# First chunk of w3·w_out in column halves, and the second chunk's transfers held behind the first 256 KB

## The chip, the core and the metric

The kernel runs on one core of a Trainium2 chip. The time is the device time of one launch in microseconds; the runs of a kernel are compared by their medians. A profiled execution is a run of its own, with its own time.

## What is computed

Linear attention without softmax for 8 batches of 8 heads (576 tokens, head dimension 64), an RMS norm over each head's 64 values scaled by `g_norm`, then a feed-forward of two projections multiplied with each other and two more matrices behind them:

```python
def _attn_ref(q, k, v, g_norm):
    kv = np.einsum('bhsd,bhse->bhde', k, v)
    out = np.einsum('bhsd,bhde->bhse', q, kv)
    rms = np.sqrt(np.mean(out * out, axis=-1, keepdims=True) + 1e-06)
    return (out / rms * g_norm).astype(np.float32)
...
    a = x @ w1
    b = x @ w2
    h = a * b @ w3
    return (h @ w_out).astype(np.float32)
```

x has 4608 rows of 512. The weights w1, w2 (512 x 1024), w3 (1024 x 1024) and w_out (1024 x 512) arrive as 64-bit floats. The kernel multiplies w3 by w_out once, at the start, and uses the product (1024 x 512) in place of the two.

## The kernel before

**Stages.** First comes the product of w3 and w_out, here called the fold. It has two halves of 512 rows of w3 (`half` 0 and 1), and each is a sum over eight chunks `c` of 128. In the fold's second half, batch 0 of the attention and the conversion of w1 and w2 are woven in. After that come nine groups of tokens: matrix products in a Strassen-Winograd form (`winograd`), with the attention of the next batch between them, and from the second group on a projection by the folded matrix in the same form (L893). This document is about the first 20 us, the beginning of the fold.

**Loads of a chunk.** `load_next` (L183 to L210) takes the next entry of `todo` and loads it into one of four `raw` buffers of 1 MB. The first eight entries are the chunks c = 0 to 7: 512 KB of w3 and 512 KB of w_out. Chunk 0 comes in four transfers of 256 KB (two of w3, two of column halves of w_out), every other chunk in two of 512 KB. All are issued at L190 by SyncE, in program order; SyncE stands still while one of them waits for its buffer or its semaphore. A semaphore is shared by transfers that lie eight apart in the program, and the later waits for the earlier: chunk 2's transfers wait for the two w3 transfers of chunk 0, and chunk 3's first for chunk 0's first w_out transfer. Four chunks are asked for at once, before anything else.

**Conversion.** The 64-bit words become 32-bit floats in `conversion`. ScalarE takes two instructions for a cut of columns (L152 into a scratch part of `ab`, L153 into `chunks`), VectorE four (L155, L159, L162, L165). `begin_next` issues ScalarE's part, `end_next` VectorE's. Chunk 0 is converted in cuts of 256, 256 and 512 columns, chunk 1 in two of 512, later chunks in one of 1024. In every chunk columns 0 to 511 are w3, 512 to 1023 are w_out. ScalarE's and VectorE's orders are written out by hand here, as are TensorE's, GpSimd's and SyncE's, so each engine works through its list in order.

**Products of a chunk.** `turn_w3` (L583) transposes the four 128 x 128 blocks of w3 on TensorE (L587) into one PSUM bank, and ScalarE copies them to `ab` (L592). `fold_chunk` (L596) multiplies them by the chunk's w_out: four matmuls `m` of 512 columns (L600), each adding to a PSUM bank of its own, so that the four banks collect the sum over the chunks. In the trace each such matmul shows as two MATMUL rows, and each `keep_warm` matmul too.

**Order on TensorE.** 14 matmuls of the identity with itself (`keep_warm`, L265), whose results nobody reads; the four transposes of chunk 0; 5 more of `keep_warm`; a transpose that makes a column of `g_norm` (L1025); three matmuls of chunk 0; the transposes of chunk 1; the fourth matmul of chunk 0; 4 of `keep_warm`; then three matmuls of chunk 1, the transposes of chunk 2, the fourth matmul of chunk 1, and so on.

**Order on ScalarE.** Chunk 0's cuts, the copy of chunk 0's transposes, chunk 1's two cuts, the copy of the `g_norm` column (L1026), chunk 2's one cut, and only then the copy of chunk 1's transposes, without which chunk 1's matmuls can't start. From there on a chunk's conversion alternates with the copy of the chunk before.

Of the kernel before, what the change touches and what calls it, by code (L numbers as in the profile page):

```python
# [11 lines left out]
FP32 = mybir.dt.float32  # L12
# [9 lines left out]
def kernel(  # L22
# [32 lines left out]
    nc = tc.nc  # L55
# [4 lines left out]
    DM = H * D  # L60
    DF = w1.shape[1]
    NP = H // 2
    KF = DF // P
    NH = KF // 2
# [11 lines left out]
    ps_at = ctx.enter_context(tc.tile_pool(name="ps_at", bufs=3, space=PSUM))  # L76
# [5 lines left out]
    def bank(pool, tag):  # L82
        return pool.tile([P, 512], FP32, name=tag, tag=tag)
# [7 lines left out]
    def load_pair(names, b, r):  # L91

        for name in names:
            t = inp.tile([P, 2, J * D], FP32, name=f"{name}_sb")
            nc.sync.dma_start(
                out=t,
                in_=dict(k=k, v=v, q=q)[name][b, 2 * r:2 * r + 2, 0:G, :].rearrange(
                    "h (p j) d -> p h (j d)", j=J
                ),
            )  # L100
            loaded[name, b, r] = t

    def load_kv_left(b):
        for t, src in zip(kv_left, (k, v)):
            nc.sync.dma_start(out=t[0:L], in_=src[b, :, G:S, :].rearrange("h p d -> p h d"))

    def load_q_left(b):
        if b % 2 == 0:
            q_left[b // 2] = inp.tile([P, H, D], FP32, name="ql_sb", bufs=1)
        nc.sync.dma_start(  # L110
            out=q_left[b // 2][(b % 2) * L:(b % 2 + 1) * L],
            in_=q[b, :, G:S, :].rearrange("h p d -> p h d"),
        )
# [64 lines left out]
    raws = []  # L178

    def raw_tile():  # L180
        return conv_pool.tile([P, 1024], w1.dtype, name="raw", bufs=RAW)

    def load_next():  # L183
        if len(raws) == len(todo):
            return
        what, i = todo[len(raws)]
        raw = raw_tile()

        def load(where, src):
            nc.sync.dma_start(out=raw[:, where].rearrange("p (c m) -> p c m", c=src.shape[1]), in_=src)  # L190

        if what == "w":
            for n, w in enumerate((w1, w2)):
                src = w[:, i * P:(i + 1) * P].rearrange("(c p) f -> p c f", p=P)
                load(slice(n * 512, (n + 1) * 512), src)
        elif what == "b":
            for h in range(2):
                src = w3[DF // 2:DF, (2 * i + h) * P:(2 * i + h + 1) * P]
                load(slice(h * 512, (h + 1) * 512), src.rearrange("(m p) f -> p m f", p=P))
        else:  # L200
            src = w3[0:DF // 2, i * P:(i + 1) * P].rearrange("(m p) f -> p m f", p=P)
            cols = w_out[i * P:(i + 1) * P, :].rearrange("p (c f) -> p c f", c=1)

            n = 1 if i else 2
            for h in range(n):
                load(slice(h * 512 // n, (h + 1) * 512 // n), src[:, h * NH // n:(h + 1) * NH // n, :])
            for h in range(n):
                f = slice(h * DM // n, (h + 1) * DM // n)
                load(slice(512 + f.start, 512 + f.stop), cols[:, :, f])
        raws.append(raw)  # L210
# [3 lines left out]
    def conversions(n):  # L214

        what, i = todo[n]
        if what == "w":
            dst = w_sb[:, i].rearrange("p w c f -> p (w c f)")

            return [conversion(n, dst, raws[n], scale=g_col)]  # L220
        if what == "b":
            return [conversion(n, chunks[:, 2 * i:2 * i + 2, 0, :], raws[n])]
        dst = chunks[:, i].rearrange("p w f -> p (w f)")
        cuts = [[0, 256, 512, 1024], [0, 512, 1024], [0, 1024]][min(i, 2)]
        return [conversion(n, dst, raws[n], slice(a, b)) for a, b in zip(cuts, cuts[1:])]

    begun = []
# [1 line left out]
    def begin_next():  # L229
        if len(begun) < len(todo):  # L230
            begun.append(conversions(len(begun)))
            for c in begun[-1]:
                next(c)

    def end_next(load=True):
        for c in begun[len(converted)]:
            all_of(c)
        converted.append(len(converted))
        if load:
            load_next()  # L240

    def all_of(steps):
        for _ in steps:
            pass


    ident = const.tile([P, P], FP32, name="ident")
# [7 lines left out]
    g_col = const.tile([P, 1], FP32, name="g_col")  # L255
# [5 lines left out]
    def keep_warm(n):  # L261

        t = bank(ps_mm, "mm")
        for _ in range(n):
            nc.tensor.matmul(t[:, 0:P], lhsT=ident, rhs=ident, start=True, stop=True)  # L265
# [315 lines left out]
    w3T = {}  # L581

    def turn_w3(half, c):  # L583
        t_ps = bank(ps_at, "at").rearrange("p (m f) -> p m f", m=NH)
        for m in range(NH):
            src = chunks[:, c, 0, m * P:(m + 1) * P]
            nc.tensor.transpose(t_ps[:, m, :], src, ident)  # L587

        w3T[half, c] = ab[c % 4 // 2][:, c % 2].rearrange(
            "p i (a f) -> p (i a) f", f=P  # L590
        )
        nc.scalar.copy(w3T[half, c], t_ps)  # L592

    sums_ps = {}

    def fold_chunk(half, c, ms):  # L596
        if c == 0 and 0 in ms:
            sums_ps[half] = [bank(ps_mm, "mm") for m in range(NH)]
        for m in ms:
            nc.tensor.matmul(  # L600
                sums_ps[half][m], lhsT=w3T[half, c][:, m, :], rhs=chunks[:, c, 1, :],
                start=(c == 0), stop=(c == KF - 1),
            )
            if c == KF - 1:
                nc.scalar.copy(w3o_sb[:, half * NH + m, :], sums_ps[half][m])
# [397 lines left out]
    chunks = fold.tile([P, KF, 2, DM], FP32, name="chunks")  # L1003
    with tc.manual_schedule(
        engines={mybir.EngineType.DVE, mybir.EngineType.Activation, mybir.EngineType.SP}
    ):
        for _ in range(RAW):
            load_next()
        nc.scalar.activation(const.tile([P, 1], FP32, name="warm"), eps_col, AF.Sqrt)
        g_row = const.tile([1, P], FP32, name="g_row")  # L1010
        for e in range(2):
            nc.scalar.dma_start(
                out=g_row[:, e * D:(e + 1) * D], in_=g_norm.rearrange("(o d) -> o d", o=1)
            )


        keep_warm(14)
        begin_next()
        end_next()
        turn_w3(0, 0)  # L1020
        keep_warm(5)
        begin_next()

        g_ps = bank(ps_at, "at")[:, 0:1]
        nc.tensor.transpose(g_ps, g_row, ident[0:1, 0:1])  # L1025
        nc.scalar.copy(g_col, g_ps)  # L1026
        for c in range(KF):

            if c == 0:
                end_next()  # L1030
                begin_next()
            else:
                begin_next()
                end_next()
            if c == 4:
                load_kv_left(0)
                load_pair("kvq", 0, 0)
            elif c == 5:
                load_pair("kvq", 0, 1)
                load_q_left(0)  # L1040
            fold_chunk(0, c, range(NH - 1))
            turn_w3(*((0, c + 1) if c + 1 < KF else (1, 0)))
            fold_chunk(0, c, [NH - 1])
            if c == 0:
                keep_warm(4)


        first = batch(0)
        first.start()
        AT = {1: 0, 2: 1, 4: 2, 5: 3}  # L1050
        norms = {}
        FIRST = len(converted) + KF - 1
        for c in range(KF):
            if c in AT:
                first.begin(AT[c])
                if AT[c] + 1 == NP:
                    load_q_left(1)
            if c - 1 in norms:
                all_of(norms[c - 1])
            if c < KF - 2:  # L1060
                begin_next()

                end_next(len(raws) < FIRST)
            elif c == KF - 2:
                run(sum_w(0))
            else:
                run(combine_x(0))
                end_next(False)
                for _ in range(3):
                    load_next()  # L1070
            fold_chunk(1, c, range(NH - 1))
            if c + 1 < KF:
                turn_w3(1, c + 1)
            fold_chunk(1, c, [NH - 1])
            if c in AT:
                if AT[c] % 2:
                    norms[c] = first.product(AT[c] // 2)
                    next(norms[c])
                    next(norms[c])
            if c - 1 in norms:  # L1080
                first.turn(AT[c - 1] - 1)
                first.turn(AT[c - 1])
# [88 lines left out]
```

## Time and profile before

| | |
|---|---|
| runs | 781.51, 781.77, 780.90, 780.05 us, median 781.21 |
| profiled execution | 782.82 us, its span 781.0 us |
| mean granted TensorE clock in it | 0.993 |
| TensorE weight loads busy | 662.7 us, 85% |
| VectorE busy | 543.6 us, 70% |
| ScalarE busy | 251.0 us, 32% |
| GpSimd busy | 129.2 us, 17% |
| share of the ended-last chain on TensorE | 90% |
| the same, on DMA | 4% |

A page of the profile gives busy times by engine, the chain of work that ended last, and groups of instructions. The chain is followed back from the last instruction to whatever released each step, so a piece of it is time that nothing else hid in that execution. The timeline of one engine lists its instructions in order: start, duration, engine, line, operation, the tile written and the tile read, shapes, how many were merged, and in brackets how long the engine sat idle before it and what ended that. Times in these views count from the span's start.

### The profile page before, as it was taken

What the parts mean: (1) busy time and instruction counts of PE and PEld (TensorE: products, weight loads), DVE (VectorE), ACT (ScalarE), POOL (GpSimd) and SP (SyncE); (2) the same over time, 40 slices, a digit from 0 to 9 for tenths busy, and PEclk for the clock granted to TensorE, in tenths of its full rate; (3) what the DMA queues carried; (4) which work ended last, traced back from release to release, by engine and by line L of the source; (5) the groups of instructions that cost most, each with busy time, mean ns of one, the idle gap of its engine ahead of it and who ended that gap; (6) DMA issues with size and microseconds to landing.
All of it is one profiled execution on the core that took longest, in us unless ns stands there. A gap on an engine that the chain in (4) does not pass through costs nothing.

```text
span 781.0 us, 14438 instructions
## 1 busy us (share of the span) xinstructions
PE 764.2 (98%) x5787; PEld 662.7 (85%) x5787; DVE 543.6 (70%) x1086; ACT 251.0 (32%) x486; POOL 129.2 (17%) x125
## 2 busy tenths in 40 slices
PE   7999999999979999999999999999999999999996
PEld 5455788888869888988998899889988988898896
DVE  6978999448579557955794778567756864494566
ACT  6687743322211332233223322332133222222120
POOL 0000000111330253024303520341144000000000
PEclk9999999999989999999999999999999999999998
DMA  9996650129987853794389458844841470064024
GB/s 321 327 340 180 194 149 28 55 88 255 256 277 249 243 128 85 282 224 115 74 288 216 119 112 271 205 111 132 275 110 42 141 244 0 1 242 143 1 65 159
DMA packets 129607, 131.76 MB, mean 169 GB/s; under 512 B 73476, under 2 KB 117508, under 8 KB 129540
## 3 DMA queue, kind: packets, MB, share of 16 engines
q1 hardware_dynamic: 127088, 116.02, 50.8%
q10 hardware_dynamic: 2452, 14.81, 5.4%
q8 instruction: 46, 0.75, 0.4%
q14 instruction: 21, 0.17, 0.1%
HBM read 100.27 MB, written 16.38 MB: 149 GB/s over the span
## 4 chain that ended last, share of the span: by engine, by line
PE 90%; DMA 4%; DVE 3%; ACT 1%; SPq 1%; issue 0%; POOL 0%; DVEq 0%; ACTq 0%; POOLq 0%
PE mm L621 57%; PE mm L893 19%; PE mm L600 7%; PE at L326 3%; PE at L409 2%; DMA raw<-w3o_l 2%; DMA raw<-in_moe_w_out_dram 1%; PE at L587 1%; DMA xn<-xT 1%; PE at L345 1%; DVE c L760 1%; DMA w3o_l<-raw 0%; DVE ab L761 0%; PE at L442 0%; DMA raw<-in_moe_w_dram 0%
## 5 line engine op out<-in xcount | busy, mean ns | idle before, releaser
L621 PE MATMUL mm<-xT,w_sb 128*128 128x256 f32 x768 | 176.2, 379 | 0.0
L621 PEld LDWEIGHTS mm<-xT,w_sb 128*128 128x128 f32 x768 | 145.5, 190 | 20.0 <-issue 0.5
L621 PE MATMUL mm<-xc,ws 128*128 128x256 f32 x576 | 132.2, 383 | 4.4 <-ACT p L634 4.4
L621 PEld LDWEIGHTS mm<-xc,ws 128*128 128x128 f32 x576 | 110.4, 192 | 20.0 <-ACT p L634 4.8
L760 DVE TENSOR_TENSOR c<-mm,u 128x512 f32<-128x512 f32 x36 | 24.9, 691 | 109.6 <-PE mm L621 109.6
L634 ACT COPY u<-mm 128x512 f32<-128x512 f32 x74 | 43.3, 585 | 142.9 <-PE mm L621 138.3
L634 ACT COPY p<-mm 128x512 f32<-128x512 f32 x74 | 43.3, 586 | 88.9 <-PE mm L621 79.4
L621 PE MATMUL mm<-xc,w_sb 128*128 128x256 f32 x288 | 69.3, 383 | 0.0
L893 PE MATMUL mm<-w3o_sb,raw 128*128 128x128 f32 x500 | 62.1, 275 | 0.5 <-DVE raw L851 0.4
L600 PE MATMUL mm<-chunks,ab 128*128 128x512 f32 x128 | 60.2, 601 | 2.3 <-DVE chunks L165 2.1
L621 PE MATMUL mm<-xT,ws 128*128 128x256 f32 x256 | 62.0, 386 | 0.0
L761 DVE TENSOR_TENSOR ab<-c 128x256 f32<-128x256 f32 x108 | 58.8, 544 | 3.0
L621 PEld LDWEIGHTS mm<-xc,w_sb 128*128 128x128 f32 x288 | 53.6, 190 | 7.8 <-ACT u L634 0.3
L893 PEld LDWEIGHTS mm<-w3o_sb,raw 128*128 128x128 f32 x500 | 58.8, 192 | 0.8 <-DVE raw L851 0.5
L286 POOL COPY qT<-q_sb 128x1024 uint16<-128x1024 uint16 x24 | 27.4, 1166 | 173.6 <-PE at L409 173.6
L621 PEld LDWEIGHTS mm<-xT,ws 128*128 128x128 f32 x256 | 48.8, 193 | 7.0
L378 DVE TENSOR_REDUCE inv<-sq 128x8 f32<-128x512 f32 (+1 forms) x40 | 23.4, 626 | 42.7 <-ACT sq L377 42.7
L760 DVE TENSOR_TENSOR c<-p,u 128x512 f32<-128x512 f32 x36 | 26.5, 736 | 28.5 <-ACT u L634 28.3
L893 PE MATMUL mm<-w3o_sb,ab 128*128 128x128 f32 x336 | 44.1, 276 | 0.5 <-DVE ab L855 0.3
L893 PEld LDWEIGHTS mm<-w3o_sb,ab 128*128 128x128 f32 x336 | 41.1, 192 | 1.2 <-DVE ab L855 0.5
L600 PEld LDWEIGHTS mm<-chunks,ab 128*128 128x128 f32 x128 | 21.9, 190 | 23.3 <-issue 15.8
L904 ACT COPY u<-mm 128x512 f32<-128x512 f32 x23 | 13.5, 586 | 87.4 <-DVE raw L917 68.4
(160 smaller groups left out, 1140.1 us busy)
## 6 DMA issues: line engine op xcount, KB each, us to landing
w3o_sb<-w3o_l SPq DMA_DIRECT2D x26, 896.0 KB, 5.3
raw<-in_moe_w_dram SPq DMA_DIRECT2D x31, 512.0 KB, 7.1
raw<-w3o_l SPq DMA_DIRECT2D x13, 896.0 KB, 4.8
w3o_sb<-w3o_l ACTq DMA_DIRECT2D x11, 896.0 KB, 4.6
k_sb<-in_k_dram SPq DMA_DIRECT2D x32, 256.0 KB, 4.1
v_sb<-in_v_dram SPq DMA_DIRECT2D x32, 256.0 KB, 4.7
q_sb<-in_q_dram SPq DMA_DIRECT2D x32, 256.0 KB, 4.2
out_dram<-raw SPq DMA_DIRECT2D x14, 512.0 KB, 3.6
```

Source lines behind the costliest of these rows:

```text
L286: nc.gpsimd.tensor_copy(to, words(src).rearrange("p n w -> p w n"))
L326: nc.tensor.matmul(kv_ps[e * D:(e + 1) * D, r - rs[0], :], lhsT=k_sb[:, e, cols] if j < J else kl[:, 2 * r + e, :], rhs=v_sb[:, e, cols] i ...
L345: nc.tensor.transpose(qt_ps[:, e, i, :], q_sb[:, e, i * P:(i + 1) * P], ident)
L378: nc.vector.tensor_reduce(out=inv[:, i], in_=sq.rearrange("p (h d) -> p h d", d=D), axis=AX.X, op=ALU.add)
L409: nc.tensor.matmul(o_ps[l][tokens, n * D:(n + 1) * D], lhsT=qT[r][rows, e, i, tokens], rhs=kv_b[rows, e, r, :], start=True, stop=True,)
L600: nc.tensor.matmul(sums_ps[half][m], lhsT=w3T[half, c][:, m, :], rhs=chunks[:, c, 1, :], start=(c == 0), stop=(c == KF - 1),)
L621: nc.tensor.matmul(ps[:, u, :], lhsT=lhsT(a_name, u, c), rhs=rhs(b_name, c),  start=(u == 0 and c == 0 and to is None), stop=(c == chunks ...
L634: nc.scalar.copy(t, ps)
L760: nc.vector.tensor_add(c, one, two)
L761: nc.vector.tensor_mul(dst, c[:, 0, :], c[:, 1, :])
L893: nc.tensor.matmul(to[:, i, :], lhsT=x[:, c, :], rhs=y[:, c, :], start=new and place // 4 not in seen, stop=(c == 1), skip_group_check=True,)
L904: nc.scalar.copy(t[:, 0:4], ps[0])
```

## The change

Chunk 0 is converted in four cuts of 256 columns. Its four matmuls of 512 columns become eight of 256: first columns 0 to 255 of all four banks, then columns 256 to 511. All eight stand ahead of chunk 1's transposes; before, the fourth matmul stood behind them. `keep_warm(4)` behind chunk 0 becomes `keep_warm(6)`, and the `g_norm` transpose with its copy moves from ahead of chunk 0's matmuls to behind that `keep_warm`. Chunk 1's `raw` buffer gets a GpSimd copy of one column (128 x 1) from chunk 0's buffer. The copy reads what the first transfer of chunk 0 brings, so GpSimd waits for that transfer; chunk 1's first transfer writes over the copied column, so SyncE waits for GpSimd at that transfer. Chunks 2 and 3 stand behind it in SyncE's list.

```diff
         raw = raw_tile()
+        if len(raws) == 1:
+            nc.gpsimd.tensor_copy(raw.bitcast(FP32)[:, 0:1], raws[0].bitcast(FP32)[:, 0:1])
...
-        cuts = [[0, 256, 512, 1024], [0, 512, 1024], [0, 1024]][min(i, 2)]
+        cuts = [[0, 256, 512, 768, 1024], [0, 512, 1024], [0, 1024]][min(i, 2)]
...
-        for m in ms:
+        n = 2 if (half, c) == (0, 0) else 1
+        for h, m in [(h, m) for h in range(n) for m in ms]:
+            cols = slice(h * DM // n, (h + 1) * DM // n)
             nc.tensor.matmul(
-                sums_ps[half][m], lhsT=w3T[half, c][:, m, :], rhs=chunks[:, c, 1, :],
-                start=(c == 0), stop=(c == KF - 1),
+                sums_ps[half][m][:, cols], lhsT=w3T[half, c][:, m, :], rhs=chunks[:, c, 1, cols],
+                start=(c == 0 and h == 0), stop=(c == KF - 1), skip_group_check=True,
             )
...
-        g_ps = bank(ps_at, "at")[:, 0:1]
-        nc.tensor.transpose(g_ps, g_row, ident[0:1, 0:1])
-        nc.scalar.copy(g_col, g_ps)
...
-            fold_chunk(0, c, range(NH - 1))
+            one = NH if c == 0 else NH - 1
+            fold_chunk(0, c, range(one))
             turn_w3(*((0, c + 1) if c + 1 < KF else (1, 0)))
-            fold_chunk(0, c, [NH - 1])
+            fold_chunk(0, c, range(one, NH))
             if c == 0:
-                keep_warm(4)
+                keep_warm(6)
+                g_ps = bank(ps_at, "at")[:, 0:1]
+                nc.tensor.transpose(g_ps, g_row, ident[0:1, 0:1])
+                nc.scalar.copy(g_col, g_ps)
```

## The prediction

> **What bounds the kernel now.** I read the page first, for which engine carries the time.
>
> ```profile
> PE 764.2 (98%) x5787; PEld 662.7 (85%) x5787; DVE 543.6 (70%) x1086; ACT 251.0 (32%) x486; POOL 129.2 (17%) x125
> ```
>
> TensorE works through 98% of the span. What is won or lost in the first 20 us reaches the end only if it moves the point from which TensorE runs without a break. The chain of waits, in order of time, gives that point:
>
> ```profile
> 1.26 3.29 DMA raw<-in_moe_w_dram
> 4.57 8.70 DMA raw<-in_moe_w_out_dram
> 13.38 1.18 ACT ab L152
> 14.55 1.06 ACT chunks L153
> 15.61 0.47 ACT ab L592
> 16.13 2.84 PE mm L600 x6
> 18.97 0.53 PE at L587 x4
> ```
>
> The columns are start, duration and what. From 16.13, chunk 1's first matmul, the chain is TensorE for some 175 us. So 16.13 is the time to watch, and what fixes it isn't chunk 0: it is the w_out transfer of chunk 2, issued at 4.57 and landed at 13.27. ScalarE converts chunk 2 (L152, L153) and only then copies chunk 1's transposes (L592). Later stretches where the chain leaves TensorE (192.76 to 218.71, for example) start from a TensorE result, so they move with it.
>
> Then ScalarE's timeline, for what stands ahead of that copy:
>
> ```profile
> 7.89 0.68 ACT L152 ACTIVATE ab<-raw 128x512 f32<-128x512 uint32 x1 [2.54 <-DMA raw<-in_moe_w_out_dram]
> ...
> 9.02 0.57 ACT L592 COPY ab<-at 128x512 f32<-128x512 f32 x1
> 9.48 0.67 ACT L152 ACTIVATE ab<-raw 128x512 f32<-128x512 uint32 x1
> ...
> 13.38 1.18 ACT L152 ACTIVATE ab<-raw 128x1024 f32<-128x1024 uint32 x1 [1.49 <-DMA raw<-in_moe_w_out_dram]
> 14.46 1.15 ACT L153 ACTIVATE chunks<-raw 128x1024 f32<-128x1024 f32 x1
> 15.52 0.56 ACT L592 COPY ab<-at 128x512 f32<-128x512 f32 x1
> ```
>
> ScalarE waits twice for w_out: 2.54 us for chunk 0's and 1.49 us for chunk 2's. The change is aimed at the first; the second sets 16.13. TensorE's timeline shows how near the two are:
>
> ```profile
> 10.96 2.81 PE L600 MATMUL mm<-chunks,ab 128*128 128x512 f32 x6 [2.14 <-DVE chunks L165]
> 13.61 0.60 PE L587 MATMUL at<-ident,chunks 128*128 128x128 f32 x4
> 14.04 1.02 PE L600 MATMUL mm<-chunks,ab 128*128 128x512 f32 x2
> 14.90 1.05 PE L265 MATMUL mm<-ident 128*128 128x128 f32 x8
> 16.13 2.84 PE L600 MATMUL mm<-chunks,ab 128*128 128x512 f32 x6 [0.17 <-ACT ab L592]
> ```
>
> TensorE idles 2.14 us before chunk 0's matmuls and 0.17 us before chunk 1's. Its own list ends at 15.95, ScalarE's copy at 16.08. An earlier chunk 0 alone is worth 0.17 us of idle time at most, and not that, because the copy ends when it does.
>
> **The transfers.** The trace records when each of a transfer's sixteen shares landed. I count these in the span's time, from the wait that ended at 13.27. Chunk 0's last transfer: fifteen shares between 5.28 and 6.29, the last at 7.80. Chunk 2's w_out: fifteen between 11.19 and 12.23, the last at 13.27. In each transfer from chunk 0's first w_out on, one share is 1.0 to 1.6 us behind the others. It fell behind once, in chunk 0's w_out (5.60 for fifteen, 7.16 for the last; one packet of 2 KB there took 1.12 us, against a mean of 0.10), and the lag stays after that. Landings come in the order of issue, and the engines are busy throughout: by the windows' DMA column 0.85 from 2 to 3 us and 0.89 to 1.14 after. So chunk 2 lands when the latest share has worked off chunks 0 to 2. Asking earlier or later changes nothing, unless a share runs dry.
>
> **The hold, costed.** Chunk 0's first transfer lands at 3.75. GpSimd has been idle since 2.48. The next row for its copy is L548, the same 128 x 1 copy: 0.19 us in the middle, 0.34 at most; the far bound is its large copy at L286, 1.17. From landing to an engine's start the rows give 0.02 (SyncE at 4.57) to 0.11 (ScalarE at 13.38). So SyncE issues chunk 1 at 3.75 + 0.11 + 0.19 + 0.02 = 4.07 instead of 2.81, 1.26 later (dearest 5.05, 2.24 later). I take 0.19, the row of the same shape. Behind it stand chunk 1's w_out (3.29 to 4.55), chunk 2's w3 (3.84 to 5.1) and w_out (4.57 to about 5.6); chunk 3 waits for chunk 0's first w_out (7.16) as before. The first issue, at 0.75, had packets moving at 1.83, 1.08 us later. Chunk 1's packets are thus there from 5.15. The fifteen faster shares are through with chunk 0 between 5.28 and 6.29, the slow one at 7.80: none runs dry. Cost: nothing, covered by chunk 0's own megabyte. Were that cover gone it would be the 1.26 us. Bounds: with the 1.17 us copy packets come at 6.1, the faster shares idle up to 0.85 us, the slowest still not at all.
>
> [...]
>
> **Chunk 0, costed.** The first w_out half (landed 7.16) no longer waits for the second (7.80). ScalarE: chunk 0's first cut of 256 ran from 3.77 to 4.53, 0.76, so the third cut runs 7.25 to 8.0, the fourth 8.05 to 8.8, and the copy (0.57) ends at 9.4; before, 9.59. VectorE: a cut of 256 took 4.24 to 5.66, 1.42, pairs 1.33 apart. Third cut done at 9.05, fourth at 10.36; before, the double cut ended at 10.81. TensorE: eight matmuls of half the columns. A row pair costs 2 x 0.43 at 512 columns in the steady stretch (3.52 for eight rows), so eight half pairs cost 3.45, as four whole ones did; I take no extra for the shorter form (bound: the 128-column row of L265 at 0.13 gives 2 x 0.13 x 16 = 4.2, 0.7 more). They run 9.45 to 12.9. Transposes 0.44, to 13.35. Six `keep_warm` at 1.05/8 per row: 1.58, to 14.9. The `g_norm` transpose 0.22, to 15.1. TensorE then has 0.85 us in hand instead of 0.13, and waits.
>
> ScalarE after its copy of chunk 0: chunk 1's first cut can't start before its w3 lands (9.19), second before w_out lands (10.54), both as before; then it waits for 13.27 as before. Copy of chunk 1 ends 16.08, matmuls at 16.13. The moved copy of the `g_norm` column (0.16) now delays chunk 3's L152 from 16.17 to 16.3; 1.14 us of ScalarE idle at 19.54 hide it. VectorE is 0.45 us earlier until chunk 2, which removes only the weight loads' wait at 18.84, behind TensorE's running matmuls.
>
> Sum: transfers 0, conversion 0 (0.45 gained off the path), TensorE 0 (0.8 gained off the path), copies 0. The span stays 781.0, and the profiled time 782.8. The unprofiled median lay 1.6 below the profiled time; the change concerns nothing that would alter that, so I forecast **781.2 us**, with its own range of 780.6 to 781.8.
>
> **The rivals.** *The late share disappears* (gain). Chunk 0's transfers have the engines to themselves until 5.15. If the 1.12 us stall came from the crowd, chunk 2 lands with its faster shares, at 12.2, the copy ends at 15.0, and TensorE, whose list now ends at 14 to 15, can use it: 1.05 less, 780.1. It is a gain only if the change itself removes the late share: in a run of the kernel before without one, chunk 0 would come early too. Against it: long packets of w_out (0.83, 0.57) appear from 3.5, before chunk 1's first packet. The farthest is set by VectorE, which converts chunks 0 and 1 from landings at 6.3 and ends at about 13.9: 2.2 us less, 779.0.
>
> *The queues run dry* (loss). If the copy on GpSimd or SyncE's wake-up takes longer, or the slow share isn't slow in ordinary runs, the shares wait for chunk 1. It decides from the point where chunk 1's first packet is later than a share's end of chunk 0, so from 6.29 when none is slow, 7.80 when one is. A full loss of the hold is 1.26, 782.5; with the dear copy 2.24, 783.4. For it: the hold is real and everything behind it in SyncE's list is late. Against it: 5.15 lies ahead of all sixteen ends.
>
> *The half-clock stretch moves.* Behind a TensorE idle of 4.39 us at 218.71 the granted clock is 0.50 until 224; eight matmul rows took 3.78 and eight 2.82 there, against 1.89 for such a group elsewhere: 2.8 us. It may fall away or come in a run by its own clock, either sign, 778.4 to 784. I see no reason why the change should steer it.
>
> **How the numbers follow.** Forecast of no change 0.62, the late share gone 0.18, queues dry 0.15, the half-clock stretch 0.05. Nothing over 0.2%, 1.56 us, comes from the forecast itself; 0.2% is about what a measurement of this kernel can tell from no change. Beyond it lie the farther half of the gain and of the loss and the clock: faster 0.13, slower 0.11, within 0.76. The range for 8 in 10 reaches to the near value of the gain and of the loss: 779.9 to 782.5.
>
> **What would show it.** Right: chunk 1's issue at about 4.1, chunk 2's w_out landed near 13.3, ScalarE's second long wait still there, chunk 0's matmuls from 9.5, TensorE idle about 1 us before chunk 1's matmuls at 16.1. Wrong: chunk 1's matmuls a microsecond earlier with no late share, or a DMA column under 0.8 around 5 to 7 us with chunk 2 landing after 14. A wait of TensorE between 20 and 180 us, where there is none now, would break the claim that the end follows 16.13 one for one.

## The result, and the profile after

The changed kernel took 782.60 us in the median (44 runs, 779.76 to 786.54), the kernel before 781.32 in the runs beside it (63 runs, 778.30 to 784.83). The ratio is 1.0018, interval 1.0010 to 1.0026: about 1.3 us slower. The ratios here are those on record, with their 95% intervals; they aren't the quotient of the two medians (1.0016 here), and in samples of 12 runs the two differ by up to 0.0010, so medians stand beside them. The forecast was 781.2, no change. The profiled execution of the changed kernel took 781.13 us, with a span of 779.3; that is less than the 782.82 and 781.0 of the one before, so a reader who compares the two profiles alone gets the wrong sign. Each is one draw from a spread of over 6 us.

The change adds three lines ahead of the functions concerned, and more further down: the matmuls of `fold_chunk` are L606 now, the copy of the transposes L595, `keep_warm` L268, SyncE's issues L193, the column copy on GpSimd L190. First the chain of waits of the changed kernel (start, duration, what):

```profile
3.78 0.02 POOLq L190
3.80 0.10 issue
3.90 0.20 POOL raw L190
4.09 0.02 issue
4.11 0.38 SPq L193
...
5.56 7.86 DMA raw<-in_moe_w_out_dram
...
13.53 1.16 ACT ab L152
14.69 1.04 ACT chunks L153
15.73 0.47 ACT ab L595
16.19 0.07 ACT g_col L1053
16.26 2.83 PE mm L606 x6
```

The hold costs what the prediction's sum said: GpSimd 0.20 us, SyncE's issue at 4.11 where it was 2.81. The chain still goes through chunk 2's w_out, landed at 13.42 (13.27 before), and chunk 1's matmuls start at 16.25 (16.13). On these two traces the change costs 0.12 us.

TensorE's timeline of the changed kernel (start, duration, line, operation, tiles, shapes, and in brackets the idle time ahead and what ended it):

```profile
9.68 3.62 PE L606 MATMUL mm<-chunks,ab 128*128 128x256 f32 x16
13.13 0.60 PE L590 MATMUL at<-ident,chunks 128*128 128x128 f32 x4
13.57 1.50 PE L268 MATMUL mm<-ident 128*128 128x128 f32 x12
15.00 0.22 PE L1052 MATMUL at<-ident,g_row 1*128 1x1 f32 x1
16.25 2.84 PE L606 MATMUL mm<-chunks,ab 128*128 128x512 f32 x6 [1.03 <-ACT g_col L1053]
```

Chunk 0's matmuls start at 9.68 instead of 10.96 with no wait ahead of them. The 2.14 us of idle time that stood there are gone, and 1.03 us stand ahead of chunk 1 instead of 0.17. The idle time has moved, from before work that doesn't set the end to before the work that does. The prediction saw this and costed it at nothing.

The transfers, in the windows of one microsecond (stretch, length, then busy time and instructions of PE, PEld, DVE, ACT and POOL, then the granted clock, the DMA engines' busy share, and GB/s). Before:

```profile
5.00:6.00 1.00, 1.00 (x8) 1.00 (x8) 0.97 (x4) 0.34 (x2) 0.00 (x0) 1.00 0.97 328
6.00:7.00 1.00, 1.00 (x11) 1.00 (x11) 0.91 (x3) 0.00 (x0) 0.00 (x0) 1.00 1.03 337
```

and after:

```profile
5.00:6.00 1.00, 1.00 (x7) 1.00 (x7) 0.97 (x4) 0.29 (x1) 0.00 (x0) 1.00 0.82 177
6.00:7.00 1.00, 1.00 (x6) 1.00 (x6) 0.93 (x4) 0.65 (x2) 0.00 (x0) 1.00 0.81 262
```

One GB/s over one microsecond is 1 KB, so 439 KB arrived in these two microseconds instead of 665, though chunk 1's first packet came at 5.19, as forecast. In windows of half a microsecond the loss lies right behind that packet: 92 GB/s from 5.5 to 6.0 us (344 before) and 180 from 6.0 to 6.5 (360 before), then 344 (313 before). The first transfers of the program rise gradually too: 75, 176, 250, 308 and 377 GB/s in the quarters of a microsecond from 1.75, in the kernel before. That is the loss the prediction excluded with "none runs dry". In this one execution it is nearly hidden, since the late share was gone: of chunk 2's w_out fifteen shares had landed by 13.14 and the last at 13.42, where it had been 12.23 and 13.27. The faster shares lost 0.9 us, and the last nearly nothing: the rival of the late share happened beside the rival of the dry queues, and the two nearly cancelled. Other executions of the same kernel had to show which of them stays.

### The profile page after: what moved, and what is told of

It is laid out like the page before. It is cut to its first block, busy times and chain, and to the rows that moved or that the text cites. A ratio compares the mean times of both kernels' runs of the same rounds, so it can differ in the third digit from the quotient of the medians.

```text
span 779.3 us, 14469 instructions
## 1 busy us (share of the span) xinstructions
PE 764.8 (98%) x5799; PEld 665.4 (85%) x5799; DVE 544.9 (70%) x1090; ACT 251.5 (32%) x488; POOL 129.5 (17%) x126
## 4 chain that ended last, share of the span: by engine, by line
PE 91%; DMA 3%; DVE 3%; SPq 1%; ACT 1%; issue 0%; POOL 0%; DVEq 0%; ACTq 0%; POOLq 0%
PE mm L627 57%; PE mm L899 20%; PE mm L606 7%; PE at L329 3%; PE at L412 2%; DMA raw<-in_moe_w_out_dram 1%; DMA raw<-w3o_l 1%; PE at L590 1%; PE at L348 1%; DVE c L766 1%; DMA xn<-xT 1%; DMA w3o_l<-raw 1%; PE at L445 0%; DMA raw<-in_moe_w_dram 0%; DVE ab L767 0%
## 5 line engine op out<-in xcount | busy, mean ns | idle before, releaser
L767 DVE TENSOR_TENSOR ab<-c 128x256 f32<-128x256 f32 x108 | 60.4, 559 | 3.0
L606 PE MATMUL mm<-chunks,ab 128*128 128x512 f32 (+1 forms) x136 | 59.9, 575 | 1.0 <-ACT g_col L1053 1.0
L606 PEld LDWEIGHTS mm<-chunks,ab 128*128 128x128 f32 x136 | 23.5, 190 | 21.2 <-issue 14.8
```

The costliest lines, as they stand in the source:

```text
L606: nc.tensor.matmul(sums_ps[half][m][:, cols], lhsT=w3T[half, c][:, m, :], rhs=chunks[:, c, 1, cols], start=(c == 0 and h == 0), stop=(c == ...
L767: nc.vector.tensor_mul(dst, c[:, 0, :], c[:, 1, :])
```

## The experiments

Five theories were kept, the last of them only from the trace of `e9_hold_1m_second` on: A, the hold lets the transfer engines run partly dry and chunk 2 lands later; B, the new order and shapes of chunk 0 cost the time; C, the difference is chance; D, the time is lost later in the program; E, an idle stretch of TensorE just ahead of chunk 1 halves its clock in some executions. All kernels here compute the full result. The runs of the kernel before that stand beside a kernel were made on the same chip as it.

**Each half of the change alone.** `e1_hold_only` is the kernel before with the three lines of the hold; `e2_halves_only` is the changed kernel without them.

```diff
         raw = raw_tile()
+        if len(raws) == 1:
+            nc.gpsimd.tensor_copy(raw.bitcast(FP32)[:, 0:1], raws[0].bitcast(FP32)[:, 0:1])
```

> The kernel before, with the GpSimd copy alone; chunk 0's cuts and matmuls stay as before. Theory A (the hold lets the transfer engines run dry): moved bytes fall to 180 to 260 GB/s between 5 and 7 us, as in the changed kernel's trace (330 before), some 0.6 us of transfer is lost for good, and the ratio to before is 1.001 to 1.002. Theory B (the new order of chunk 0 costs): 1.000. Theory C (chance between executions; neither part costs): 1.000.

> The changed kernel without the GpSimd copy: four cuts, eight half matmuls, moved g_norm transpose, six keep_warm, but chunk 1 asked for at 2.8 us as before. Theory A: 0.999 to 1.000, moved bytes at 330 GB/s between 5 and 7 us. Theory B: 1.001 to 1.002, all of the loss. Theory C: 1.000.

Hold alone: 1.0001 (0.9987 to 1.0016), 781.79, 12 runs. Halves alone: 0.9997 (0.9983 to 1.0011), 781.57, 12 runs. The halves cost nothing that can be measured. Two more samples of them below, with 9 idle matmuls, are both 0.9993, and none of these 36 runs lies over 784 us: B falls. The hold alone can't be told from nothing either, so A's 1.001 to 1.002 missed, though its windows show 199 and 327 GB/s for 5 to 6 and 6 to 7 us, as A expected. Taken one at a time the parts don't add up to the loss of the whole. Nor do their single traces part them: chunk 2's w_out landed at 13.46 in both, and chunk 1's matmuls start at 16.28 with the hold alone and at 16.27 with the halves alone, which have no hold.

**A later hold.** The copied column is taken from a later transfer: chunk 0's second (`e3_hold_512k`), or its fourth (`e7_hold_1m`, `e9_hold_1m_second`, `e10_hold_1m_third`).

```diff
-            nc.gpsimd.tensor_copy(raw.bitcast(FP32)[:, 0:1], raws[0].bitcast(FP32)[:, 0:1])
+            nc.gpsimd.tensor_copy(raw.bitcast(FP32)[:, 0:1], raws[0].bitcast(FP32)[:, 512:513])
```

The 1 MB form has column 1536 there.

> The changed kernel with the hold doubled: the GpSimd copy reads what chunk 0's second transfer brings (landed at 4.5 us instead of 3.75), so chunk 1 is asked for at about 4.9 us instead of 4.1. Theory A: the engines are dry 0.7 to 0.8 us longer, the ratio rises by 0.0009 to about 1.0027, chunk 2's w_out lands at 14.0 to 14.3 us. Theories B and C: no different from the changed kernel, 1.0018 or 1.000.

> The changed kernel with the hold lengthened to all of chunk 0: the GpSimd copy reads what its fourth transfer brings (landed at 6.9 to 7.8 us), so chunk 1 is asked for at 7.3 to 8.2 us instead of 4.1. Theory A: the engines stand still for some 2 to 3 us, chunk 2's w_out lands 3.2 to 4 us later, at 16.5 to 17.5, chunk 1's matmuls start at 19.3 to 20.3, and the ratio to before is 1.0045 to 1.006. Theories B (chunk 0's new order) and C: 1.000 to 1.002, as for the changed kernel.

> A second trace of the longest hold. Its timed runs lie 5 us above the kernel before, its first trace showed chunk 1's matmuls only 1.5 us late, and that trace was of its fastest run. Theory A: chunk 1's matmuls start at 17.3 to 20.3 us, and a run slower than 784 us shows them late by as much as it is slow. Theory D (the loss sits behind the start, at the w1 and w2 transfers around 83 us or in the stretch from 208 to 262 us): chunk 1's matmuls again near 17.3, and the time is lost later.

> A third trace of the longest hold, for the same question. Theory A: matmuls of chunk 1 late by as much as the run is slow. Theory D: near 17.3 us, with the loss behind 60 us.

512 KB: 1.0020 (1.0005 to 1.0035), 782.76, 12 runs, up to 787.10. 1 MB: 1.0064 (1.0039 to 1.0090), 785.86, 6 runs, up to 790.10. The windows of the 1 MB form show what running dry is:

```profile
5.00:6.00 1.00, 1.00 (x7) 1.00 (x7) 0.97 (x4) 0.90 (x4) 0.00 (x0) 1.00 0.20 76
6.00:7.00 1.00, 1.00 (x8) 1.00 (x8) 0.93 (x5) 0.74 (x3) 0.19 (x1) 1.00 0.00 0
7.00:8.00 1.00, 1.00 (x12) 1.00 (x11) 0.93 (x4) 0.00 (x0) 0.00 (x0) 1.00 0.59 190
```

The 1 MB form is plainly longer, which is A's sign; 256 and 512 KB can't be told apart by their times (1.0016 to 1.0020 and 1.0020). In the trace of the 512 KB form chunk 2's w_out landed at 14.78, behind A's 14.0 to 14.3, and chunk 1's matmuls start at 17.61. In the first trace of the 1 MB form it landed at 14.44, well ahead of A's 16.5 to 17.5, because chunk 0 itself was in at 5.96 and SyncE issued chunk 1 at 6.31. But chunk 1's matmuls start at 17.31, 18.19 and 18.35 in the three traces of the 1 MB form, 1.2 to 2.2 us after the 16.13 of the kernel before, while its median is 5.0 us over the 780.86 of the kernel before beside it. Something costs more than the late start. The second trace of this form, an execution of 786.56 us, shows it. TensorE's timeline:

```profile
8.44 3.69 PE L606 MATMUL mm<-chunks,ab 128*128 128x256 f32 x16
14.13 0.66 PE L590 MATMUL at<-ident,chunks 128*128 128x128 f32 x4 [2.00 <-DVE chunks L165]
...
18.19 4.85 PE L606 MATMUL mm<-chunks,ab 128*128 128x512 f32 x6 [1.35 <-ACT g_col L1053]
```

and its windows of 3.41 us. The granted clock changes at 15.45, 22.27 and 223.66 us there, 2 and 59 such steps apart:

```profile
12.03:15.45 3.42, 1.42 (x13) 1.32 (x13) 3.32 (x7) 1.56 (x3) 0.00 (x0) 1.00 1.05 380
15.45:18.86 3.41, 2.06 (x9) 1.58 (x8) 2.88 (x5) 3.30 (x5) 0.00 (x0) 0.50 1.07 387
18.86:22.27 3.41, 3.41 (x5) 1.33 (x4) 3.34 (x5) 1.60 (x2) 0.00 (x0) 0.50 1.06 381
22.27:25.68 3.41, 3.41 (x12) 1.58 (x11) 2.42 (x3) 2.16 (x3) 0.00 (x0) 1.00 1.05 373
```

In 12.03 to 15.45 TensorE was busy for 1.42 of 3.42 us, 0.41. The two stretches behind it ran at a granted clock of 0.50, and six rows of chunk 1 took 4.85 us instead of 2.84. From the start of chunk 1's matmuls to the transposes behind them are 22.88 - 18.19 = 4.69 us here and 2.68 in the third trace of the same kernel, which kept its clock: 2.0 us lost on the path. At 64 us the same instruction of ScalarE, counted from the end of the program, is 3.96 us behind the profiled execution of the kernel before: 2.06 for the later start of chunk 1, and the rest for the clock.

**Repeats.** `e5_before_again` is the kernel before against itself; `e4_changed_again` is the changed kernel once more, beside e1 to e3; `e6_before_third`, `e8_changed_third`, `e11_changed_fourth` and `e12_before_fourth` are one execution each of the two kernels, for the traces.

> The changed kernel once more, on the chip of the other three and with a second trace. Theory A: 1.0018 again, moved bytes low between 5 and 7 us again, and chunk 2's w_out landed between 13.0 and 13.8 us. Theory B: 1.0018, with the landing where it was before. Theory C: the ratio lies nearer to 1.000 than to 1.0018.

> The kernel before, unchanged, timed against itself and with a second trace. It gives how far two samples of the same kernel lie apart (ratio 1.000, and how wide the interval is), and where chunk 2's w_out lands and chunk 1's matmuls start without the hold. Theory A (the hold lets the transfer engines run dry): bytes between 5 and 7 us at 300 GB/s or more, chunk 2 landed at 12.2 to 13.5 us, chunk 1's matmuls at 15.1 to 16.3. Theory C (chance): the landing scatters as far as in the two traces of the changed kernel, 13.4 to 13.8 us and beyond.

> A third trace of the kernel before, for the scatter of chunk 2's landing and of chunk 1's first matmul. Theory A: the mean start of chunk 1's matmuls over the three traces of before lies 0.3 to 1.2 us ahead of the 16.26, 16.28 and 16.56 us of the traces with the hold. Theory C: no difference.

> A third trace of the changed kernel. Theory A: bytes under 300 GB/s between 5 and 7 us, chunk 2's w_out landed at 13.3 to 14.3 us, chunk 1's matmuls at 16.2 to 17.1. Theory C: landing anywhere between 12.2 and 14.3, as in the kernel before.

> A fourth trace of the changed kernel. Theory A: bytes under 300 GB/s on the mean of 5 to 7 us, chunk 1's matmuls at 16.2 to 17.1 us; a run over 783 us shows its loss there. Theory C: chunk 1's matmuls at 15.7 to 16.2 as in the kernel before.

> A fourth trace of the kernel before. Theory A: chunk 1's matmuls at 15.7 to 16.2 us, bytes over 300 GB/s on the mean of 5 to 7 us. Theory C: 16.2 to 16.7, as with the hold.

Changed again: 1.0016 (0.9999 to 1.0032), 782.10. Before against itself: 1.0016 (1.0004 to 1.0028), 781.72 against 780.86. The second is a warning: a sample of 12 runs differs from its own kernel by as much as the effect sought, and the interval shown for one sample is too narrow. So C is not refuted by any one of these runs, only by all of them: the changed kernel was 1.0016 to 1.0020 each time it was timed, in 68 runs. By the medians alone the three samples are 1.28, 0.53 and 1.49 us over the kernel before.

The traces (later ones, `e16_changed_fifth` among them, are used here too) give:

| | before, four traces | changed, five traces |
|---|---|---|
| GB/s, 5 to 6 us | 328, 345, 266, 279 | 177, 231, 209, 163, 219 |
| GB/s, 6 to 7 us | 337, 364, 357, 315 | 262, 302, 300, 280, 239 |
| chunk 2's w_out landed | 13.27, 12.86, 12.86, 13.77 | 13.42, 13.77, 13.85, 13.88, 13.87 |
| chunk 1's matmuls start | 16.13, 15.73, 15.72, 17.26 | 16.25, 16.56, 16.62, 16.65, 16.69 |
| idle ahead of chunk 0's matmuls | 2.14, 0.94, 1.32, 1.94 | none |
| idle ahead of chunk 1's matmuls | 0.17, 0.54, 0.16, none | 1.03, 2.26, 2.27, 2.53, 1.65 |

Every changed trace has fewer bytes in these two microseconds than every trace of before. The same holds when all traces are taken: at least 594 KB in the eight without a hold, at most 533 KB in the eight with the hold of 256 KB. The means of the start are 16.55 and 16.21. The 17.26 is `e12_before_fourth`, where A's expectation missed; it shows what a halved clock does in the kernel before. Its TensorE timeline:

```profile
10.73 4.12 PE L600 MATMUL mm<-chunks,ab 128*128 128x512 f32 x6 [1.94 <-DVE chunks L165]
...
17.26 2.74 PE L600 MATMUL mm<-chunks,ab 128*128 128x512 f32 x6
```

and its windows, cut at the clock's changes, 12.09 and 15.51 us, and 3.41 us ahead of the first:

```profile
8.68:12.09 3.41, 1.47 (x4) 0.70 (x5) 3.27 (x8) 3.12 (x7) 0.00 (x0) 1.00 1.03 370
12.09:15.51 3.42, 3.42 (x9) 1.76 (x8) 3.14 (x6) 1.64 (x2) 0.00 (x0) 0.50 1.06 388
```

Behind a window that was 0.43 busy, chunk 0 runs slow. But TensorE would have waited for chunk 1 anyway, and longer than in the other three, since chunk 2's w_out landed late here, at 13.77. In those three, chunk 1's matmuls start 2.75 to 2.77 us after ScalarE's first instruction on chunk 2, which began at 13.88 here: without the slow clock chunk 1 would have started at about 16.64, an estimate. So about 0.6 us of the time lost reaches chunk 1, and nothing slow is left by then. With 16.64 in place of 17.26 the mean start of before is 16.06, and the changed kernel's 16.55 is 0.5 us later. For comparison the profiled execution of the kernel before, in which the idle stretch of 2.14 us is longer but lies across a window's edge, at 12.51 us, 60 steps of 3.41 us ahead of that trace's first change of clock at 217.32:

```profile
9.11:12.51 3.40, 1.55 (x4) 0.87 (x5) 3.26 (x8) 2.78 (x7) 0.00 (x0) 1.00 1.06 392
12.51:15.93 3.42, 3.42 (x17) 2.01 (x16) 3.35 (x6) 2.55 (x3) 0.00 (x0) 1.00 1.08 382
```

0.46 busy, and the clock stays. On the grid that each trace's own changes of clock give, one edge lies anywhere between 10.34 us (e17) and 13.59 (e10) in the 20 traces, so the same idle time lies inside one window in some executions and across two in others. If the clock goes by these windows, that makes a tail, and there is one: over 784 us were 15 of the 70 runs of the changed kernel, and 5 of the 183 of the kernel before. But most of it isn't shown to come from the clock. All runs of before moved up by 1.05 us, the distance of the two medians, would put about 9 of 70 there. And the one execution of the changed kernel over 784 us that has a trace, the 784.21 of `e16_changed_fifth`, kept its full clock at chunk 1, started it at 16.69 like the others, and lost its time behind 206 us: at 207 us it is 0.58 us behind the profiled execution of before, the other four 0.87 on the mean, and at the end it is 2.6 us behind those four.

Three of the changed traces have more than 2.2 us of idle time ahead of chunk 1, and all three kept their clock. In the windows of `e4_changed_again` the first two are those of its clock, placed by the later changes at 220.47 and 223.87 us, 60 and 61 steps of 3.41 us behind 15.65; the third is as long and begins at 13.00, so that 2.11 us of the idle stretch lie in it:

```profile
12.24:15.65 3.41, 2.06 (x17) 1.85 (x17) 2.54 (x5) 1.91 (x3) 0.00 (x0) 1.00 1.05 392
15.65:19.07 3.42, 2.51 (x6) 1.20 (x7) 3.35 (x5) 3.13 (x5) 0.00 (x0) 1.00 1.07 378
13.00:16.41 3.41, 1.30 (x12) 1.09 (x10) 2.54 (x5) 2.54 (x4) 0.00 (x0) 1.00 1.07 393
```

An edge of the window at 15.65 divides the idle stretch, so the windows are 0.60 and 0.73 busy; started 0.8 us later, the window would have been 0.38 busy, less than any that kept its clock.

**Theory E alone: more or less to do ahead of chunk 1.** Only the count of idle matmuls behind chunk 0 is changed, so neither transfers nor conversions are touched. E's figures in the expectations are those of e9 and e12: 2.00 us idle out of 3.42 and 1.94 out of 3.41, and behind them 6.82 and 3.42 us at a granted clock of 0.50.

```diff
             if c == 0:
-                keep_warm(6)
+                keep_warm(10)
```

`e13_changed_warm10` has 10, `e14_changed_warm1` has 1, `e16_changed_fifth` is the changed kernel beside them. `e15_halves_warm9` and `e17_halves_warm9_second` have no hold and 9. The median of the kernel before was 780.52 beside the first four (31 runs) and 781.23 beside e17 (23 runs).

> The changed kernel with ten keep_warm matmuls behind chunk 0 instead of six, 1.05 us more of TensorE work in the idle time ahead of chunk 1, which was 1.03 to 2.53 us in four traces. Theory E (an idle stretch of about 1.9 us or more within one 3.4 us window halves TensorE's clock for 3.4 or 6.8 us, and the change moved such a stretch to where nothing hides the slow matmuls): the idle time falls to 0 to 1.5 us, the slow tail over 784 us (11 of 44 runs of the changed kernel) goes, ratio 1.0000 to 1.0008. Theory A alone (late transfers): the ratio stays at that of the changed kernel, with its tail. Theory C: no order between the four.

> The changed kernel with one keep_warm matmul behind chunk 0 instead of six: 1.3 us less of TensorE work ahead of chunk 1, so an idle time of 2.3 to 3.8 us. Theory E: nearly every run falls to half clock there, chunks 1 and 2 run slow for 3.4 to 6.8 us, 1.7 to 3.4 us are lost, the ratio is 1.003 to 1.0045 and most runs lie over 783.5 us. Theory A alone: keep_warm matmuls stand in idle time, so nothing changes against the changed kernel. Theory C: the same.

> The changed kernel beside the three on the same chip. Theory E: a quarter or more of its runs over 784 us, ratio 1.001 to 1.0025, between the ten and the one keep_warm. Theory A alone: equal to both. Theory C: no order.

> Four cuts and eight half matmuls without the hold, and nine keep_warm matmuls behind chunk 0 (0.79 us more than six). Both theories A and E: no dry engines, no idle stretch over 1 us ahead of chunk 1; ratio 0.9985 to 1.0000, the shortest of the four. Theory C: no order.

> Four cuts and eight half matmuls without the hold, nine keep_warm matmuls behind chunk 0, once more on another chip or day. Theories A and E: ratio 0.9985 to 1.0000 again, no run over 784 us; chance would put it as often above 1.000.

| kernel | ratio | median | highest | runs over 784 |
|---|---|---|---|---|
| hold, 10 idle matmuls (e13) | 1.0001 (0.9990 to 1.0012) | 781.11 | 782.21 | 0 of 12 |
| hold, 6: the changed kernel (e16) | 1.0020 (1.0007 to 1.0032) | 782.01 | 784.21 | 1 of 12 |
| hold, 1 (e14) | 1.0037 (1.0022 to 1.0052) | 784.17 | 785.23 | 6 of 8 |
| no hold, 9 (e15) | 0.9993 (0.9981 to 1.0005) | 780.57 | 781.74 | 0 of 12 |
| no hold, 9, again (e17) | 0.9993 (0.9980 to 1.0006) | 780.82 | 783.16 | 0 of 12 |

With the hold, the less TensorE has to do ahead of chunk 1, the longer the program takes, although the work taken away is of no use to anyone. TensorE's timeline with 10:

```profile
13.55 2.40 PE L268 MATMUL mm<-ident 128*128 128x128 f32 x20
15.88 0.22 PE L1052 MATMUL at<-ident,g_row 1*128 1x1 f32 x1
16.80 2.84 PE L606 MATMUL mm<-chunks,ab 128*128 128x512 f32 x6 [0.70 <-ACT g_col L1053]
19.48 0.60 PE L590 MATMUL at<-ident,chunks 128*128 128x128 f32 x4
```

and with 1:

```profile
13.60 0.39 PE L268 MATMUL mm<-ident 128*128 128x128 f32 x2
13.91 0.22 PE L1052 MATMUL at<-ident,g_row 1*128 1x1 f32 x1
16.86 5.43 PE L606 MATMUL mm<-chunks,ab 128*128 128x512 f32 x6 [2.72 <-ACT g_col L1053]
22.12 0.60 PE L590 MATMUL at<-ident,chunks 128*128 128x128 f32 x4
```

Chunk 1's matmuls start at the same time, 16.80 and 16.86. With 10 they take 2.68 us to the next transposes, with 1 5.26: 2.58 us lost. The windows with 1, cut at the clock's changes, 15.26 and 22.09 us, and in steps of 3.41 us:

```profile
11.85:15.26 3.41, 1.38 (x9) 0.82 (x7) 3.19 (x7) 1.79 (x4) 0.00 (x0) 1.00 1.04 390
15.26:18.67 3.41, 1.81 (x2) 0.84 (x3) 3.26 (x4) 3.37 (x6) 0.00 (x0) 0.50 1.07 378
18.67:22.09 3.42, 3.42 (x5) 1.24 (x4) 3.35 (x5) 0.42 (x1) 0.00 (x0) 0.50 1.06 374
```

The first is 0.40 busy, then comes half clock, and it stays for a second window, behind the first, which was 0.53 busy. This is E, on the path: the medians of e14 and e13 lie 3.1 us apart, and their intervals don't overlap. Against the sample e16, e13 gains 0.9 us in the median, with chunk 1 starting no earlier (16.80 against 16.69); their intervals overlap, and 0.9 us is what two samples of one kernel differed by. E's forecast of a quarter of e16's runs over 784 us missed: it was 1 of 12.

**The same remedy in the kernel before.** `e18_before_warm9` is the kernel before with 9 idle matmuls instead of 5 ahead of chunk 0, where its idle time is.

```diff
         turn_w3(0, 0)
-        keep_warm(5)
+        keep_warm(9)
         begin_next()
```

> The kernel before with nine keep_warm matmuls instead of five ahead of chunk 0's matmuls, 1.05 us more of TensorE work in the idle time there (0.9 to 2.1 us in four traces, behind which one trace ran at half clock). Theory E: the half clock no longer falls there, which touched a quarter of the runs at about 1.3 us each, so 0.9985 to 1.0000. Without theory E: 1.000.

Measured: 1.0015 (1.0001 to 1.0029), 781.92, 12 runs. E's expectation missed. Its trace has no idle time over 0.2 us and no half clock there, and chunk 1 at 15.70, as early as any trace of the kernel before. Either this is the scatter that e5 showed, the same 1.0015, or the additional matmuls hold chunk 0 up in executions in which the first 14 idle matmuls end late (at 8.29 us in its own trace, at 6.91 in e12). Nothing here tells which.

## Why the prediction was wrong

By its own steps:

- *What bounds the kernel.* Right for the start: in every one of the 20 traces ScalarE begins chunk 2 within 0.12 us of its w_out's landing, and chunk 1's matmuls wait for what follows, except in three (e12, e17, e18) where TensorE's own list ends as late. *The hold's issue*: 4.07 forecast, 4.11 measured. *First packets*: 5.15 forecast, 5.19 measured. *Shape of chunk 0's matmuls*: 3.45 forecast for the eight half pairs, 3.45 measured (9.68 to 13.13). *End of TensorE's list*: 15.1 forecast, 15.22 measured, which is partly luck: chunk 0's matmuls started at 9.68 because the first 14 idle matmuls took 6.34 us (5.17 before), not because of ScalarE's copy, and in the other four changed traces the list ended between 14.1 and 15.05. The sum itself has a slip: from 15.1 to ScalarE's copy at 16.08 is 0.98 us; the 0.85 it gives as "in hand" is the distance to the old end of the list, 15.95.
- *"None runs dry. Cost: nothing, covered by chunk 0's own megabyte."* Wrong, the first failing step, and the one that the traces show. The prediction asked whether the first new packet comes before the last old one. It does, and still the bytes of the two microseconds fell in every trace. The cover was counted as whole until its end, and the new transfer as whole from its first packet; in the trace the rate was 92 and 180 GB/s in the halves of a microsecond from 5.5, against 344 and 360. Chunk 2's w_out landed at 13.76 on the mean of five changed traces and at 12.93 on that of eight traces without a hold (the four of before, the three of halves alone and with 9, e18's). So about 0.8 of the hold's 1.3 us come back at the far end (0.6 against the four traces of before alone), and 0.34 (16.55 - 16.21) at chunk 1's start, or 0.5 with the clock's part taken out of e12. Of the 1.26 us that the prediction gave for a hold without that cover, 0.6 to 0.8 came back.
- *"TensorE then has 0.85 us in hand instead of 0.13, and waits."* Costed at nothing, the second failing step in mechanism, though its price in this kernel isn't shown. The idle time was 1.03 to 2.53 us, because the list ended early and the release came late. Such idle time wasn't free in e9 and e14: with 2.00 and 2.03 us of it inside one window of 3.42 and 3.41 us, the granted clock was 0.50 from 15.45 and 15.26 us on, and still when the matmuls on the path began. The price there was 2.0 and 2.6 us. In the five traces of the changed kernel itself it wasn't paid, so how much of the 1.3 us it makes up isn't shown. The prediction had the half clock as a rival, but put it only at 217 to 224 us and saw "no reason why the change should steer it". The change moves TensorE's idle time to a place where a slow clock cost e14 the whole 2.58 us.
- *The claim that "the end follows 16.13 one for one".* Wrong too. The prediction named the sign that would break this, a wait of TensorE between 20 and 180 us, and it came. `e4_changed_again` has one of 0.83 us, `e8_changed_third` one of 0.52, e9 and e10 0.54 and 0.44; no trace without a hold has any. In e4 ScalarE's conversion of w1 and w2 waits for its transfer (81.98 in the kernel before, no wait), and TensorE for what follows:

```profile
83.76 1.14 ACT L152 ACTIVATE ab<-raw 128x1024 f32<-128x1024 uint32 x1 [1.34 <-DMA raw<-in_moe_w_dram]
89.46 1.99 PE L627 MATMUL mm<-xc,ws 128*128 128x256 f32 x8 [0.83 <-ACT p L640]
```

From 77 to 112 us the five changed traces lose 0, 1.06, 0.75, 0.53 and 0.13 us more than the kernel before's first trace; its other three lose none, and e2, e15 and e18, which have no hold either, 0.10 to 0.22. So about 0.5 us on the mean is lost a second time, in e4 to a late transfer. Nothing here tells whether the hold is the reason, or why only in some executions.
- *The late share.* The rival came true in the first trace (6.96 instead of 7.80) and hid the loss there. The other changed traces, with chunk 2 at 13.77 to 13.88, show no gain.
- *B and D.* The halves cost nothing (0.9997, and 0.9993 twice). The difference in span of the two first traces, 1.7 us in the changed kernel's favour, comes from one stretch, from ScalarE's instruction at 205.76 (205.78 after) to its copy at 260.18 (258.53): 54.43 us before and 52.76 after. Over the traces of the two kernels the same stretch takes 52.1 to 54.4, with no order between them, so this part of D is chance.

How the 1.3 us divide is only estimated. The same instruction of ScalarE, counted from the end of the program, can be compared over the traces. At 28 us the five changed traces are 0.33 us behind the four of before on the mean, at 207 us 0.80: a third of a microsecond from the start and half a microsecond from 77 to 112 us. Behind 207 us, stretches that scatter in both kernels hide any further difference. The runs agree with a loss in most executions: in the runs of the result the lowest quarter ends at 781.28 (780.42 before), the median is 782.60 (781.32), and the highest quarter begins at 784.00 (782.21), so 0.9 us lie in the lower part and more in the upper. For the clock an estimate from the traces is this, if the clock halves behind every window at most 0.43 busy, as it did behind those of e9, e12 and e14, and if a window can begin anywhere: to leave a window at most 0.43 busy, 0.57 of 3.41 us, 1.94, must be idle inside it. A stretch of 2.26, 2.27 or 2.53 us does that for 52%, 53% or 60% of the window's possible starts, one of 1.03 or 1.65 for none. Over the five changed traces that is 0.33, at 2.0 to 2.6 us each 0.7 to 0.9 us on the mean; for the kernel before, with 2.14 and 1.94 us of idle time in two of four traces, 0.23 at 0.6 us, about 0.1. That is what E could cost. That none of the three stretches was punished is a chance of about 1 in 11 by the same figures, so E's real part may well be smaller.

What stays open. No trace of the changed kernel itself caught the halved clock at chunk 1. That it happens there rests on e9 and e14, and on the order of e13, e16 and e14. The hold alone was 1.0001, so its part isn't shown by itself; that the loss needs the hold rests on the three samples without it. The slow rise behind chunk 1's first packet is seen in the traces, but why the engines rise slowly wasn't tested, and neither was the wait at 83 us. e18 stays unexplained. The variant without a hold and with 9 idle matmuls is the best seen, twice 0.9993, but both intervals hold 1, and by the medians it is 0.05 us over the kernel before and 0.41 under: it isn't shown to be faster than the kernel before.

## What to carry to other kernels

Before idle time of TensorE is costed at nothing, look at what runs behind it: in e9 and e14 some 2 us of it in the 3.41 us ahead of a change to a granted clock of 0.50 went with another 2.0 and 2.6 us lost on the path, and in e13 cheap matmuls that nobody reads shortened the gap to 0.70 us. Don't count a transfer that is issued later as covered by another until the other's last byte: here chunk 1's first packet came at 5.19 us, 5.15 forecast, and still 439 KB arrived in two microseconds instead of 665. Compare the bytes per microsecond, not the first and last packets. One profile each, or 12 runs each, can't settle 0.2% here. Compare quartiles as well as the median before a tail is given a cause of its own, and profile one of the slow executions. When a prediction names a sign of being wrong, look for that sign in every trace, far from the change too.

## What the runs showed of the hardware

- In e9, e12 and e14 the changes of the granted clock at 12 to 23 us and at 220 to 227 lie whole steps of 3.41 us apart (59 from 22.27 to 223.66 us in e9, 60 from 15.51 to 220.31 in e12, 58 from 22.09 to 220.06 in e14). On the grid that each trace's changes give, one edge lies between 10.34 us (e17) and 13.59 (e10) in the 20 traces.
- Of the windows on that grid, seven a trace from 3.51 to 6.76 us on, those at full clock that were 0.40, 0.41 and 0.43 busy (e14, e9, e12) were followed by a granted clock of 0.50; the next fuller one, 0.46 (the profiled execution of before), wasn't, nor was any other. In these three traces full clock came back behind a window that was busy throughout (from 18.67 us in e14, 18.86 in e9, 12.09 in e12); behind 0.60 (e9) and 0.53 (e14) it stayed 0.50.
- Behind chunk 1's first packet at 5.19 us the profiled execution after moved 92 and 180 GB/s in the halves of a microsecond from 5.5, against 344 and 360 before.
- The same kernel, in two samples on one chip, 12 and 17 runs, differed by 1.0016 (1.0004 to 1.0028).
